# Twenty-eight instead of twenty-four half slabs of expert weights queued behind attention units 0 to 19

## The chip, the cores and the metric

One Trainium2 chip, and one of its cores. The core has five engines that run side by side: TensorE (PE, with its weight loads as PEld), VectorE (DVE), ScalarE (ACT), GpSimd (POOL) and SyncE (SP), which here issues all DMAs. Sixteen DMA engines move the data between the chip's memory and SBUF. The metric is the device time of one execution in microseconds, as the median of several runs; less is better.

## The reference

Three stages, one behind the other: a linear attention with decay over blocks of 64, a soft mixture of experts in which 32 slots go through 8 experts, and a layer of the form g(x w_in) w_out with g(h) = h - tanh(h).

```python
def _attn_ref(q, k, v, lam):               # 4 x 8 heads x 768 x 64
    for b in range(nb):                    # 12 blocks of 64
        intra = (qb @ kb^T * Dmask) @ vb
        inter = (qb * lam_pow) @ kv_state
        out[:, :, sl] = intra + inter
        kv_state = lam_block * kv_state + (kb * rev_pow)^T @ vb

def _moe_ref(x, phi, w1, w2):              # x 3072 x 512, w1 8 x 512 x 1024, w2 8 x 1024 x 512
    logits = x @ phi                       # 3072 x 32
    d = softmax of logits over the tokens
    slot_input = d.T @ x
    for e in range(E):                     # 4 slots each
        slot_out[e] = max(slot_input[e] @ w1[e], 0) @ w2[e]
    return softmax of logits over the slots @ slot_out

def _moe2_ref(x, w_in, w_out):             # 512 x 2048, 2048 x 512
    h = x @ w_in
    return (h - tanh(h)) @ w_out
```

## The kernel before

**Attention.** Queries are taken in 24 units: chunk c of 128 positions (six of them) and batch b (four), u = 4c + b, all eight heads at once. A unit needs a tile of q and k (`qk`, 512 KB, L237), one of v (256 KB, L244) and, for 14 of the units, one of k turned (256 KB, L242); for the six units of `TURN_K` TensorE makes the turned k itself (L250), and the last chunk needs none. `scores(u)` multiplies q and k (L285), `attend(u)` applies them to v and adds the state's part (L302, L309), and updates the state (L318). `route(u)` turns the result for the experts' routing (L343), and routing sums run along with the attention. Three buffers each hold `qk`, `v` and `k`.

**Order.** The program is written in the order in which each engine runs it. Pass u of the loop issues `qk` of unit u + 3, then `fill(FILL[u])`, then k and v of unit u + 3; it holds the scores of unit u + 1 and the attend of unit u. SP is one queue in program order: an issue that has to wait for a buffer holds up everything behind it. The v of unit u + 3 uses the buffer of unit u, so it waits for unit u's attend. A DMA also waits for the one that was issued eight before it to land.

**Expert weights.** There are 32 tiles of 1 MB (two of w1 and two of w2 for each of the 8 experts), each loaded by two DMAs of 512 KB, called halves here. `fill(n)` queues up to n halves, in the order of the experts, as long as a ring has a free tile. The rings: `a` with 3 tiles and `b` with 12, there from the start; `d` with one, in memory that is free once the state is no longer updated (opened behind pass 19); `e` with one, in that of `qk` (opened behind pass 22); `c` with 4, in the rest of the attention's memory (opened at its end). So at most 30 halves can be queued before pass 20, 32 before pass 23. Behind the attention, a tile that an expert has used is filled again (`freed`), with the later experts' weights and then with slabs of w_in and w_out.

**Experts and main stage.** For each expert e, `expert1(e)` (L576, names `hp<-w`) multiplies the slots by w1, and `expert2(e - 1)` (L600, `op<-w`) the earlier expert's hidden values by w2. Then slabs of w_in and w_out, which come as 64-bit numbers (`wi`, `wo`, 512 KB a load), are decoded by GpSimd (`top`, L117) and VectorE (`wif`, `wf`, L121), and the main stage works through 96 chunks with TensorE, ScalarE and VectorE (L795 to L828). The slabs go through ring `a` of three tiles, so that a load there waits for an earlier slab's decode.

Of the kernel before, what the change touches and what calls it, by code (L numbers as in the profile page):

```python
# [63 lines left out]
LINEAR = 43, 47  # L64
CHECK = 57, 59, 63
TURN_K = [0, 1, 2, 6, 11, 16]
FILL = [2, 1, 1, 2, 1, 1, 1, 1, 1, 1, 2, 1, 1, 1, 1, 2, 1, 1, 1, 1, 3, 3, 6, 8]
RING = dict(a=3, b=12, d=1, e=1, c=4)
RING_OF = "a" * 3 + "b" * 12 + "de" + "c" * 4 + "a" * 3 + "b" * 8

# [2 lines left out]
def tile_main(ctx, tc, qkv, lam, phi, w1, w2, w_in, w_out, out):  # L73
# [107 lines left out]
    def fill(most=100):  # L181
        while most and (half or weight_loads and free[ring_next()]):
            if half:
                next(half[0])
                half.pop()
            else:
                f, *a = weight_loads.pop()
                steps = f(*a)
                next(steps)
                half.append(steps)  # L190
            most -= 1
# [18 lines left out]
    with pool("att_out") as att_out:  # L210
# [226 lines left out]
        for u in range(-1, NU):  # L437
            if 3 <= u + 3 < NU:
                load_unit(u + 3, 0)
            if u >= 0:  # L440
                fill(FILL[u])
            if 3 <= u + 3 < NU:
# [705 lines left out]
```

## Time and profile before

| | |
|---|---|
| median of 3 runs | 317.36 us (317.2 to 318.54) |
| profiled execution, its own time | 314.61 us |
| its span | 312.8 us |
| TensorE busy | 294.9 us (94%) |
| VectorE, ScalarE, GpSimd busy | 180.8, 134.0, 111.8 us |
| moved by DMA | 79.77 MB, mean 255 GB/s |
| chain that ended last, by engine | PE 55%, DMA 27%, DVE 8%, issue 4% |
| granted TensorE clock, mean | 0.994 of full speed |

The profile is of one execution, in microseconds from the start of its span; 1.8 us of its time lie outside the span. The attention runs to about 108 us, the routing's end to 116, the experts to 157, the main stage from there to the end. The share of busy time on TensorE is high in all of them, since its instructions are pipelined and their ends are modelled, so what a stage waits for is to be read from the instructions themselves. A DMA share is the mean over the core's 16 DMA engines and can come out a little over 1 in a short stretch.

### The profile page before, as it was taken

The page shows a single profiled execution, that of the slowest core. Times are in us where ns is not written, and L with a number is a line of the kernel's source. Part 1 is how long each engine was busy: PE and PEld are TensorE (multiplying, and loading weights), DVE is VectorE, ACT ScalarE, POOL GpSimd, SP SyncE. Part 2 cuts the span into 40 slices and gives each one's busy share as a digit, 9 for nine tenths or more (in the row PEclk, how much of TensorE's full clock was granted, in tenths as well). Part 3 has the DMA queues.
Part 4 walks back from the last instruction along what each step waited for, and adds up shares of the span by engine and source line. Part 5 has one row for each costly group of instructions (what it writes and reads, how often), then busy time and mean ns, then how long its engine had stood idle before and what let it go on. Part 6 is the DMA issues. An engine that isn't in the chain of part 4 may idle for free.

```text
span 312.8 us, 7421 instructions
## 1 busy us (share of the span) xinstructions
PE 294.9 (94%) x2999; PEld 213.3 (68%) x2999; DVE 180.8 (58%) x329; ACT 134.0 (43%) x280; POOL 111.8 (36%) x163
## 2 busy tenths in 40 slices
PE   8989999999999999997989889999999899999991
PEld 7868787878787774442366567777754677787771
DVE  4844444554544244510069758597772877968782
ACT  1434333233433423321249578586633544454420
POOL 3346766577573014010376345677500001000000
PEclk9999999999999999999999999999999999999997
DMA  6999999999999999999999847563000030303254
GB/s 202 375 397 389 396 377 327 394 369 316 404 336 376 395 402 399 394 397 400 392 348 324 312 148 272 176 237 127 2 2 0 2 134 0 134 2 134 81 188 141
DMA packets 33255, 79.77 MB, mean 255 GB/s; under 512 B 3648, under 2 KB 3904, under 8 KB 33216
## 3 DMA queue, kind: packets, MB, share of 16 engines
q1 hardware_dynamic: 33216, 79.25, 68.8%
q8 instruction: 25, 0.41, 0.5%
q14 instruction: 14, 0.11, 0.1%
HBM read 72.95 MB, written 6.29 MB: 253 GB/s over the span
## 4 chain that ended last, share of the span: by engine, by line
PE 55%; DMA 27%; DVE 8%; issue 4%; POOL 1%; SPq 1%; ACT 1%; DVEq 0%; POOLq 0%; ACTq 0%
PE ops L820 22%; DMA w<-in_w 16%; DMA qk<-in_qkv 7%; PE dps L795 6%; PE sc L285 6%; PE xp L309 5%; DMA wi<-in_w_in 3%; DVE r L813 3%; PE xnp L343 3%; PE xp L302 3%; PE up L318 2%; DVE part L828 2%; PE ops L1056 1%; PE ap L387 1%; PE qp L872 1%
## 5 line engine op out<-in xcount | busy, mean ns | idle before, releaser
L820 PE MATMUL ops<-wr,r 128*128 128x512 f32 (+1 forms) x388 | 109.0, 397 | 1.2 <-ACT part L826 0.9
L820 PEld LDWEIGHTS ops<-wr,r 128*128 128x128 f32 x388 | 72.3, 188 | 22.2 <-ACT part L826 3.1
L799 ACT ACTIVATE s<-dps 128x512 f32<-128x512 f32 x96 | 56.9, 603 | 53.8 <-PE dps L795 51.5
L813 DVE SCALAR_TENSOR_TENSOR r<-dps,mt,s 128x512 fp32r<-128x512 f32 x89 | 64.9, 746 | 19.7 <-ACT s L799 18.9
L795 PE MATMUL dps<-c,ms 128*128 128x512 f32 x96 | 39.5, 425 | 3.8 <-DVE r L813 1.9
L289 DVE TENSOR_TENSOR at<-sc,dtab 128x512 f32<-128x512 f32 x48 | 30.9, 684 | 13.9 <-PE sc L285 13.9
L257 POOL TENSOR_TENSOR qs<-qk,ql 128x512 f32<-128x512 f32 x20 | 25.8, 1288 | 30.0 <-DMA qk<-in_qkv 26.5
L345 ACT COPY xn<-xnp 128x512 f32<-128x512 f32 x24 | 14.1, 586 | 41.7 <-PE xnp L343 41.7
L285 PE MATMUL sc<-qk 64*128 64x128 f32 x384 | 27.9, 285 | 1.8 <-DMA qk<-in_qkv 1.7
L285 PEld LDWEIGHTS sc<-qk 64*128 64x128 f32 x384 | 23.3, 187 | 8.1 <-issue 5.0
L795 PEld LDWEIGHTS dps<-c,ms 128*128 128x128 f32 x96 | 17.9, 188 | 15.2 <-DVE r L813 7.4
L309 PE MATMUL xp<-at,v 128*64 128x128 f32 x384 | 26.3, 279 | 0.0
L264 POOL TENSOR_TENSOR kc<-k,dtab 128x512 f32<-128x512 f32 x20 | 21.2, 1059 | 12.7 <-PE up L318 5.5
L312 ACT COPY xt<-xp 128x256 f32<-128x256 f32 x48 | 17.8, 373 | 16.5 <-PE xp L309 16.0
L309 PEld LDWEIGHTS xp<-at,v 128*64 128x64 f32 x384 | 20.5, 136 | 4.1 <-issue 3.8
L324 DVE TENSOR_TENSOR st<-up,sd 128x256 f32<-128x256 f32 x16 | 6.8, 425 | 26.0 <-PE up L318 23.7
L828 DVE TENSOR_TENSOR part<-ops,part 128x512 f32<-128x512 f32 (+1 forms) x29 | 17.9, 665 | 0.9 <-PE ops L1056 0.9
L576 PE MATMUL hp<-w,si 128*32 128x256 f32 x256 | 16.1, 383 | 2.4 <-DMA w<-in_w 2.4
L600 PE MATMUL op<-w,hz 128*32 128x512 f32 x128 | 16.5, 594 | 0.0
L117 POOL CAST top<-wo 128x512 f16<-128x512 bf16 x16 | 14.9, 953 | 4.2 <-DMA wo<-in_w_out 2.2
L117 POOL CAST top<-wi 128x512 f16<-128x512 bf16 x16 | 14.1, 896 | 6.2 <-DMA wi<-in_w_in 5.6
L121 DVE SCALAR_TENSOR_TENSOR wif<-wi,top 128x512 uint32<-128x512 uint32 x16 | 13.2, 833 | 5.4 <-POOL top L117 5.4
(181 smaller groups left out, 340.7 us busy)
## 6 DMA issues: line engine op xcount, KB each, us to landing
w<-in_w SPq DMA_DIRECT2D x64, 512.0 KB, 9.9
qk<-in_qkv SPq DMA_DIRECT2D x24, 512.0 KB, 7.2
wi<-in_w_in SPq DMA_DIRECT2D x16, 512.0 KB, 4.8
wo<-in_w_out SPq DMA_DIRECT2D x16, 512.0 KB, 4.3
v<-in_qkv SPq DMA_DIRECT2D x24, 256.0 KB, 6.4
out<-part SPq DMA_DIRECT2D x23, 256.0 KB, 2.2
k<-in_qkv SPq DMA_DIRECT2D x14, 256.0 KB, 7.8
out<-part SPq DMA_DIRECT2D x2, 128.0 KB, 3.5
```

What stands on the lines that cost most here:

```text
L117: nc.gpsimd.tensor_copy(out=every(top().bitcast(F16), 2, 1)[:, sl], in_=every(raw().bitcast(BF16)[:, 4:], 4, 0)[:, sl])
L257: nc.gpsimd.tensor_tensor(out=qs_t[u], in0=qk_t[u][:, 0], in1=ql, op=ALU.mult)
L264: nc.gpsimd.tensor_tensor(out=kc_t[u], in0=k_t.pop(u).rearrange("p (h d) -> p h d", h=H), in1=kd, op=ALU.mult)
L285: nc.tensor.matmul(sc[h2][:, p], qk[sl, 1, p], qk[sl, 0, p], start=True, stop=True)
L289: nc.vector.tensor_tensor(out=by_head(at_t[u], h2), in0=sc[h2], in1=by_head(dtab, h2), op=ALU.mult)
L309: nc.tensor.matmul(at_head(p, h2), v[:, h * DH:(h + 1) * DH], at[:, h], start=c == 0 and p < 2, stop=True, skip_group_check=True)
L312: nc.scalar.copy(xt_t[u][:, h2], xp[h2])
L795: nc.tensor.matmul(d_t[n], ms[:, f * P:(f + 1) * P], c4[:, c], start=True, stop=True)
L799: nc.scalar.activation(out=s, in_=d_t[n], func=AF.Square, scale=math.sqrt(1.0 / 3))
L813: nc.vector.scalar_tensor_tensor(out=r_t[n], in0=d, scalar=mt[:, f, NS:], in1=s, op0=ALU.add, op1=ALU.mult)
L820: nc.tensor.matmul(op, r_t[n][:, t * P:(t + 1) * P], wr_t[f // 2][:, f % 2, sl], start=first, stop=last)
L828: nc.vector.tensor_tensor(out=pt, in0=op, in1=pt, op=ALU.add)
```

## The change

One table changes: how many halves each pass may queue. The sum of the first twenty passes goes from 24 to 28: pass 3 queues one fewer, passes 5, 6, 13, 17 and 19 one more each, and pass 21 is allowed two instead of three. Passes 20 to 22 queued the last eight of the first 32 halves (three, three, two); now pass 20 queues three, pass 21 one and pass 22 none, because the rings are full.

```diff
 TURN_K = [0, 1, 2, 6, 11, 16]
-FILL = [2, 1, 1, 2, 1, 1, 1, 1, 1, 1, 2, 1, 1, 1, 1, 2, 1, 1, 1, 1, 3, 3, 6, 8]
+FILL = [2, 1, 1, 1, 1, 2, 2, 1, 1, 1, 2, 1, 1, 2, 1, 2, 1, 2, 1, 2, 3, 2, 6, 8]
 RING = dict(a=3, b=12, d=1, e=1, c=4)
```

Which half of which tile a pass loads shifts along, and with it the numbers in the tiles' names. Nothing moves on the other engines. The rows below are SP's queue in program order; in a name such as `w2_0_1_407`, 2 says w2, 0 the expert, 1 the tile, and the last number is the buffer's. `L237` loads q and k, `L242` the turned k, `L244` v, `L156` and `L165` halves of w1 and w2.

SP in passes 5 and 6, from q and k of unit 8 to those of unit 10, before:

```order
L237 DMA qk_502<-in_qkv 128x1024
L165 DMA w2_0_1_407<-in_w2 128x2x512
L242 DMA k_505<-in_qkv 128x512
L244 DMA v_507<-in_qkv 128x512
L237 DMA qk_576<-in_qkv 128x1024
L156 DMA w1_1_0_578<-in_w1 128x1024
L242 DMA k_580<-in_qkv 128x512
L244 DMA v_582<-in_qkv 128x512
L237 DMA qk_641<-in_qkv 128x1024
```

The same stretch after:

```order
L237 DMA qk_500<-in_qkv 128x1024
L165 DMA w2_0_1_502<-in_w2 128x2x512 x2
L242 DMA k_505<-in_qkv 128x512
L244 DMA v_507<-in_qkv 128x512
L237 DMA qk_576<-in_qkv 128x1024
L156 DMA w1_1_0_578<-in_w1 128x1024 x2
L242 DMA k_581<-in_qkv 128x512
L244 DMA v_583<-in_qkv 128x512
L237 DMA qk_642<-in_qkv 128x1024
```

Each pass queues two halves instead of one between a load of q and k and the next one.

SP in passes 17 to 20, from the weights of pass 17 on, before:

```order
L165 DMA w2_2_0_1314<-in_w2 128x2x512
L244 DMA v_1409<-in_qkv 128x512
L237 DMA qk_1478<-in_qkv 128x1024
L165 DMA w2_2_1_1480<-in_w2 128x2x512
L244 DMA v_1482<-in_qkv 128x512
L237 DMA qk_1541<-in_qkv 128x1024
L165 DMA w2_2_1_1480<-in_w2 128x2x512
L244 DMA v_1544<-in_qkv 128x512
L237 DMA qk_1603<-in_qkv 128x1024
L156 DMA w1_3_0_1605<-in_w1 128x1024 x2
L156 DMA w1_3_1_1608<-in_w1 128x1024
```

After:

```order
L165 DMA w2_2_1_1317<-in_w2 128x2x512
L156 DMA w1_3_0_1412<-in_w1 128x1024
L244 DMA v_1414<-in_qkv 128x512
L237 DMA qk_1483<-in_qkv 128x1024
L156 DMA w1_3_0_1412<-in_w1 128x1024
L244 DMA v_1486<-in_qkv 128x512
L237 DMA qk_1545<-in_qkv 128x1024
L156 DMA w1_3_1_1547<-in_w1 128x1024 x2
L244 DMA v_1550<-in_qkv 128x512
L237 DMA qk_1609<-in_qkv 128x1024
L165 DMA w2_3_0_1611<-in_w2 128x2x512 x2
L165 DMA w2_3_1_1614<-in_w2 128x2x512
```

Passes 17 and 19 queue two halves instead of one, and the weights run four halves ahead by then; in pass 20 the first half of the second w2 tile of expert 3 (ring `d`) stands ahead of the last v, where a half of w1 of that expert stood.

## Rows read from the trace of the kernel before

**Rows 1.** Chain of waits, in order of time: start us, us, what.

```profile
55.25 8.25 DMA qk<-in_qkv
63.55 1.16 PE sc L285 x16
...
146.37 10.65 DMA wi<-in_w_in
157.07 0.87 POOL top L117
```

**Rows 2.** TensorE, experts 6 and 7: start, us, engine, line, operation, names, count, [idle before].

```profile
140.20 1.93 PE L576 MATMUL hp<-w,si 128*32 128x256 f32 x32
141.96 1.90 PE L600 MATMUL op<-w,hz 128*32 128x512 f32 x16
...
144.28 0.38 PE L588 MATMUL ht<-cst,hr 128*128 128x128 f32 x2
145.21 0.64 PE L576 MATMUL hp<-w,si 128*32 128x256 f32 x8 [0.55 <-DMA w<-in_w]
...
149.41 1.90 PE L600 MATMUL op<-w,hz 128*32 128x512 f32 x16
```

**Rows 3.** Stretches: us, busy of five engines, granted clock, DMA share, GB/s.

```profile
18.00:45.00 27.00, 25.45 (x463) 20.91 (x460) 11.84 (x24) 8.87 (x23) 16.97 (x18) 1.00 1.03 389
45.00:51.00 6.00, 6.00 (x103) 4.40 (x98) 2.51 (x5) 3.33 (x11) 5.04 (x6) 1.00 0.88 316
...
69.00:78.00 9.00, 9.00 (x168) 7.65 (x168) 4.00 (x8) 3.25 (x7) 6.81 (x8) 1.00 0.95 312
78.00:90.00 12.00, 12.00 (x227) 9.50 (x215) 6.29 (x13) 4.86 (x14) 6.72 (x8) 1.00 1.03 399
90.00:99.00 9.00, 9.00 (x170) 7.63 (x168) 3.94 (x9) 3.15 (x10) 5.01 (x5) 1.00 0.92 328
99.00:156.00 57.00, 54.09 (x649) 28.52 (x645) 16.68 (x50) 16.73 (x40) 9.27 (x29) 1.00 1.04 397
```

**Rows 4.** SP's waits: engine, line, releaser: us in total, times, longest.

```profile
SPq L244 <- PE up L318: 34.4, 19, 3.4
```

**Rows 5.** SP: issues of q and k for units 10, 20, 21, 23.

```profile
37.48 0.42 SPq L237 DMA_DIRECT2D qk<-in_qkv  x1
...
81.80 0.42 SPq L237 DMA_DIRECT2D qk<-in_qkv  x1
...
85.72 0.38 SPq L237 DMA_DIRECT2D qk<-in_qkv  x1
...
94.24 0.61 SPq L237 DMA_DIRECT2D qk<-in_qkv  x1
```

**Rows 6.** DMA issues: KB, us to landing; rows 5's four, then 107.7 and 162.4 us.

```profile
qk<-in_qkv SPq DMA_DIRECT2D x1, 512.0 KB, 7.2
...
qk<-in_qkv SPq DMA_DIRECT2D x1, 512.0 KB, 7.7
...
qk<-in_qkv SPq DMA_DIRECT2D x1, 512.0 KB, 7.0
...
qk<-in_qkv SPq DMA_DIRECT2D x1, 512.0 KB, 6.0
...
w<-in_w SPq DMA_DIRECT2D x1, 512.0 KB, 8.4
...
wi<-in_w_in SPq DMA_DIRECT2D x1, 512.0 KB, 3.9
```

**Rows 7.** TensorE: first scores of units 10, 20, 21 and 23.

```profile
45.53 1.16 PE L285 MATMUL sc<-qk 64*128 64x128 f32 x16
...
89.94 1.16 PE L285 MATMUL sc<-qk 64*128 64x128 f32 x16
...
93.71 1.16 PE L285 MATMUL sc<-qk 64*128 64x128 f32 x16
...
102.72 1.16 PE L285 MATMUL sc<-qk 64*128 64x128 f32 x16
```

## The prediction

> **What bounds the kernel now.** I read the chain of waits first, then TensorE's instructions at the end of the expert stage, then the DMA share by stretch, then the landing of single loads.
>
> The chain runs on TensorE through the attention, with a few loads of q and k in it: the load issued at 55.25 landed 8.25 us later, and the scores started 0.05 us after that [rows 1]. So a load's time to landing counts from the start of its issue, and the attention's operands sometimes come last already. Behind the attention the chain is DMA up to 157 us: the first slab of w_in, issued at 146.37, landed 10.65 us later and released the first decode [rows 1].
>
> TensorE gives the other view of that place. Expert 6 goes through its first product and on to the next in 1.76 us (140.20 to 141.96); expert 7, whose turn came with the transposes at 144.28, reached the same point at 149.41, after four waits on weights, the first of 0.55 us [rows 2]. Up to expert 6 the stage runs at TensorE's pace, and at expert 7 TensorE catches up with the DMA. Without waits expert 7 would have started 0.31 us behind the transposes (as expert 6 did behind its own) and been through at 144.28 + 0.31 + 1.76 = 146.35. **At most 149.41 - 146.35 = 3.06 us are to be had there**, and only if both sides come earlier: the weights, and TensorE itself.
>
> The DMA had room in the attention and none behind it. The share is 1.03 to 1.04 where the queue is full (389 GB/s in 18 to 45 us, 399 in 78 to 90, 397 in 99 to 156), and there are three dips: 0.88 and 316 GB/s, 0.95 and 312, 0.92 and 328 [rows 3]. SP doesn't look far ahead: 19 loads of v wait for the state update of an earlier unit, 34.4 us in sum [rows 4], and all that SP issues later stands behind them. If little is queued per unit, the DMA runs dry.
>
> **The change, part by part.** It computes nothing new. 64 halves of weights are loaded before and after; a half costs 0.524 MB / 397 GB/s = 1.32 us of DMA [rows 3]. Against the kernel before, SP is one half behind after pass 3, level after pass 5, one ahead from pass 6, two from 13, three from 17, four from 19, and level again at pass 22. A half that pass u adds goes out behind the q and k of unit u + 3 and ahead of those of unit u + 4.
>
> *Pass 3's half taken out.* The queue is full there, so the half moves to pass 5 for nothing: 0. No scores stall that this could free; the loads for units 6 to 8 land earlier than needed.
>
> *Four halves ahead.* Two prices have to be found: how much the DMA makes up in the dips (what the end of the weights gains), and how long TensorE stands still for late q and k. For the second, the slack of a load is the start of its scores less its issue less its time to landing: unit 10 has 45.53 - 37.48 - 7.2 = 0.85 us, unit 20 0.44, unit 21 0.99, unit 23 2.48 [rows 5 to 7]. Read in the same way, units 17, 18, 19 and 22 have 2.07, 1.50, 1.17 and 1.15, unit 11 with its transposes 0.96, and unit 14 none [rows 1].
>
> How much a dip takes is not shown by any row; two readings bound it. By bytes, against 389 GB/s, the dips lose 6 x 73/389 = 1.13, 9 x 77/389 = 1.78 and 9 x 61/389 = 1.41 us. By DMA share, against 1.035, they are free for 0.90, 0.74 and 1.00 us [rows 3].
> - By bytes: pass 6's half makes unit 10 wait 1.32 - 0.85 = 0.47, and the other 0.85 goes in the first dip. Pass 13's half goes in the second, behind slacks of 2.07 and 1.50. Pass 17's makes unit 21 wait 1.32 - 0.99 = 0.33; the 0.99 left and pass 19's 1.32 are under unit 23's slack once the last dip has taken 1.41. Stalls 0.80; made up 0.85 + 1.32 + 1.41 = 3.58.
> - By share: 0.47 again; of pass 13's half 0.58 stays, which unit 20 feels by 0.14; then 0.44 + 1.32 - 0.99 = 0.77 at unit 21; the rest, 2.31 - 1.00 = 1.31, is under 2.48. Stalls 1.38; made up 0.85 + 0.74 + 1.00 = 2.59.
>
> I take 1.2 us of stalls, nearer to the share, since that is the row that says whether a DMA engine was free. The Trainium skill speaks against that choice ("Perfetto Trace Analysis", Identifying the Most-Contended Engine): it wants the bytes, since the occupancy of 16 DMA engines misleads. By it the stalls would be 0.8 and the gain 0.4 us more; here bytes and share dip in the same three places and differ in depth.
>
> *The rings.* By pass 22 both kernels have queued 32 halves, and the next go out when attention memory is free. SP then stands with less behind it. Before, the first load past the attention's end took 8.4 us to land; one that found little queued took 3.9 [rows 6]. So there are 4.5 us of queue to use up, against 3.58 + 0.80 or 2.59 + 1.38: it doesn't run dry, by little. The sixteenth tile, now asked for in pass 20, waits for the last state update, which was over before the v ahead of it could go out: 0.
>
> *Sum.* TensorE starts the experts 1.2 us later (0.80 to 1.38), runs through expert 7 without the waits, and is 3.06 - 1.2 = 1.9 us earlier behind it (1.68 to 2.26). The weights and w_in, 2.6 to 3.6 us ahead, allow that. What is late next is the decode: it starts from the same w_in load and TensorE's next product, both moved, and from there slab loads wait for decoded slabs, so all shifts together. On the profiled execution 314.61 becomes 312.7; the median of the runs is 317.36, 2.75 above, and becomes **315.5 us**.
>
> **The rivals.**
>
> *No room.* The dips are not idle in the sense that counts, and nothing is made up. Then each half ahead is paid where the slack ends: 0.47 at unit 10, 0.85 at unit 14, 0.15, 0.73 and 0.77 at units 19 to 21, 2.97 in sum. Expert 7 no longer waits, since TensorE is that much later itself: 3.06 - 2.97 = 0.1, and the weights land when they did. 317.3 us. For it: with a share of 0.88 to 0.95 most engines are busy in a dip, and a load has landed only when its last part has. Against it: bytes fall by 16 to 20% there. The Trainium skill bears on it ("DMA: Bandwidth & Descriptors", Why a DMA increments its semaphore by 16 and not by 1): up to 16 engines finish independently and only the full count means landed. By that, a dip in the mean may hide one late engine; no row here tells the engines apart.
>
> *Slower.* Every half ahead is paid in full on TensorE: a stall delays the attend, the attend delays the v that SP waits for [rows 4], and the next q and k go out as late as the stall was long, so no slack returns. Price 4 x 1.32 = 5.28, less 3.06: 2.2 us, 319.6 us. It decides from stalls over 3.06 us; over 4.65 it can be measured. Against it: the loads of units 22 and 23 had 1.15 and 2.48 us left, and a stalled TensorE gives the queue time to drain.
>
> *It changes nothing at the end*, because the queue runs dry at the attention's end and the halves gained are lost again. Price: 317.4. The 4.5 us speak against it; I count it with no room.
>
> **How the numbers follow.** About 0.5% (1.6 us) is what a measurement here can tell from no change. Forecast, stalls of 0.80 to 1.38: 0.45, and its times, 315.1 to 315.7, are just faster by that. No room, the dry queue, and stalls between 1.5 and 4.6: 0.38, all within 0.5%. Slower: 0.17. So faster 0.45, same 0.38, slower 0.17. The range runs from 314.6, where only unit 10 stalls (3.06 - 0.47 gives 314.8) with a little for the spread of the runs, to 318.8, inside the slower case; about 1 in 20 lies below, 3 in 20 above.
>
> **What would show it.** Right: the three dips filled to a share near 1.03; the scores of units 10 and 21 waiting for q and k, with 0.8 to 1.4 us more of that in sum; expert 0 starting that much later; no wait on weights in expert 7; the first w_in slab landing over 2 us earlier. No room: dips as before, or filled with the landings no denser, and stalls near 3 us. Wrong altogether: stalls over 3 us, or a gap in the DMA at 105 to 112 us, or the 1.9 us present at 157 and gone by the first outputs.

## The result and the profile after

The kernel after took 314.39 us (313.24 to 315.38, 4 executions) beside 317.49 us (317.2 to 318.54, 4) for the kernel before: a ratio of 0.9895 [0.9848, 0.9943]. Two further comparisons of 12 executions each gave 315.20 beside 316.48 us, 0.9973 [0.9935, 1.001], and 315.14 beside 316.41, 0.9971 [0.9933, 1.0009]. Over all executions the medians are 315.11 us (28, from 311.9 to 317.7) and, beside all the experiments but without the four of the first comparison, 316.55 us (121, from 313.3 to 319.93). So the change is worth about 1.4 us or 0.45%, less than half of what the first comparison shows. Ratios here leave out executions more than 1.5% above their kernel's fastest; medians and the counts by clock further below are over all executions.

The first median lies 0.2 us below the range that was given, the median of all 28 lies 0.4 us below the forecast of 315.5. That nearness says little: the profiled execution on which the sum rests was not like most, and larger errors nearly cancel, as the last part shows.

The profiled execution of the kernel after took 315.38 us (span 313.6), which is *more* than the 314.61 of the one before. Two executions decide nothing; what they show is where the time lies. First the DMA in the three dips of [rows 3], by the stretches of the kernel after (us, busy of the five engines, granted clock, DMA share, GB/s):

```profile
45.00:51.00 6.00, 5.63 (x105) 4.75 (x105) 2.77 (x5) 2.94 (x10) 3.57 (x4) 1.00 1.01 382
69.00:78.00 9.00, 8.43 (x146) 7.02 (x144) 4.18 (x7) 3.25 (x7) 4.16 (x6) 1.00 1.04 383
90.00:99.00 9.00, 8.40 (x169) 7.07 (x165) 3.94 (x9) 2.51 (x6) 4.29 (x5) 1.00 1.01 390
```

The dips are gone: 316, 312 and 328 GB/s have become 382, 383 and 390. Where they were, TensorE now stands a little. Four of the scores that wait for q and k, of units 9, 10, 17 and 21, in TensorE's order of time (start, us, engine, line, operation, names, count, [idle before]):

```profile
41.22 1.16 PE L285 MATMUL sc<-qk 64*128 64x128 f32 x16 [0.31 <-DMA qk<-in_qkv]
46.42 1.16 PE L285 MATMUL sc<-qk 64*128 64x128 f32 x16 [0.35 <-DMA qk<-in_qkv]
77.87 1.16 PE L285 MATMUL sc<-qk 64*128 64x128 f32 x16 [0.57 <-DMA qk<-in_qkv]
95.71 1.16 PE L285 MATMUL sc<-qk 64*128 64x128 f32 x16 [0.60 <-DMA qk<-in_qkv]
```

Their sum up to 118 us, from the waits of the kernel after (us in total, times, longest):

```profile
PE sc L285 <- DMA qk<-in_qkv: 4.2, 7, 1.0
```

In the kernel before that sum is 1.7 us in 3 waits. Of the difference, 2.5 us, 0.69 is a wait of unit 0's scores, which delays nothing (they start at 6.08 us, beside 6.06 before); the other 1.8 us are most of what reaches the experts. TensorE's expert 0, expert 7 and first product of the main stage, kernel after:

```profile
117.81 1.93 PE L576 MATMUL hp<-w,si 128*32 128x256 f32 x32
...
146.29 0.38 PE L588 MATMUL ht<-cst,hr 128*128 128x128 f32 x2
146.60 1.30 PE L576 MATMUL hp<-w,si 128*32 128x256 f32 x16
148.54 0.64 PE L576 MATMUL hp<-w,si 128*32 128x256 f32 x8 [0.64 <-DMA w<-in_w]
149.83 0.64 PE L576 MATMUL hp<-w,si 128*32 128x256 f32 x8 [0.65 <-DMA w<-in_w]
150.29 1.90 PE L600 MATMUL op<-w,hz 128*32 128x512 f32 x16
...
159.11 1.10 PE L743 MATMUL mp__2401<-wif,so 128*32 128x128 f32 x16
```

and the first and the last of these places in the kernel before:

```profile
115.80 1.93 PE L576 MATMUL hp<-w,si 128*32 128x256 f32 x32
...
158.23 1.11 PE L743 MATMUL mp__2401<-wif,so 128*32 128x128 f32 x16
```

Expert 0 starts 117.81 - 115.80 = 2.01 us later. Expert 7 has two waits on weights, 1.29 us, instead of the four of [rows 2], and the stretch from expert 0 to the main stage is 41.30 us long instead of 42.43. From there to the end of the span it is 154.5 us in this execution and 154.6 in that one, and between 154.1 and 155.2 in every trace of this study: what stands at the main stage's first product stands at the end, to within about 1 us. So two marks tell nearly the whole time of a trace, the start of expert 0 (called E below) and the start of the main stage (M).

Two repeats of the kernel after came out better in their traces: E 116.33 and M 155.75 (no wait left in expert 7), and E 117.48 and M 157.36 (one wait of 0.30 us). The first of them is of the fastest of the 28 executions, 311.9 us.

Why weights still come late in this trace, though SP is four halves ahead, shows at the attention's end. The stretch of 108 to 118 us, before:

```profile
108.00:118.00 10.00, 9.79 (x118) 7.01 (x116) 3.38 (x16) 2.87 (x11) 1.93 (x6) 1.00 1.04 399
```

and after, its first 8 us in pieces of 2 us:

```profile
108.00:110.00 2.00, 2.00 (x36) 1.63 (x36) 0.00 (x0) 1.20 (x3) 0.00 (x0) 1.00 0.79 305
110.00:112.00 2.00, 2.00 (x42) 1.68 (x41) 0.36 (x2) 0.72 (x2) 0.00 (x0) 1.00 0.69 233
112.00:114.00 2.00, 1.79 (x16) 1.27 (x18) 1.22 (x7) 1.53 (x6) 0.00 (x0) 1.00 0.92 268
114.00:116.00 2.00, 2.00 (x19) 1.19 (x11) 0.91 (x3) 0.55 (x3) 0.00 (x0) 1.00 0.85 237
```

The queue has run low: 233 to 305 GB/s for 8 us, where the kernel before moves 399. SP's waits say what it stood at. Between 100 and 125 us, after (engine, line, releaser: us in total, times, longest):

```profile
SPq L156 <- DMA v<-in_qkv: 5.9, 2, 5.6
SPq L156 <- PE hp L576: 4.3, 1, 4.3
SPq L165 <- PE op L600: 2.8, 1, 2.8
```

Before, most of SP's waiting there is for a weight load issued eight earlier to land, that is, for a full queue:

```profile
SPq L165 <- DMA w<-in_w: 6.9, 8, 1.0
SPq L156 <- DMA w<-in_w: 5.3, 7, 0.9
SPq L156 <- PE xp L309: 2.5, 1, 2.5
SPq L156 <- PE hp L576: 0.7, 1, 0.7
```

After, SP stands because memory isn't free: all the halves that rings `a`, `b` and `d` hold, 32, are queued early, the next place is the attention's (the 5.6 us end when the last v has landed), and then that of tiles which TensorE has yet to use (4.3 and 2.8 us). The chain of waits of the kernel after runs through just that place (start us, us, what):

```profile
108.69 1.05 PE xp L309 x16
109.80 0.33 SPq L156
...
113.35 0.62 SPq L156
114.01 12.22 DMA w<-in_w
126.25 10.52 DMA w<-in_w
136.78 10.44 DMA w<-in_w
147.24 10.65 DMA wi<-in_w_in
```

From the last attend over SP's issues into four loads, of which the last is the first slab of w_in. Set beside [rows 1], that slab is issued 0.87 us later than before and takes the same 10.65 us.

### The profile page after: what moved, and what is told of

It reads as the page before. It is cut to its first block, busy times and chain, and to the rows that moved or that the text cites. A ratio compares the mean times of both kernels' runs of the same rounds, so it can differ in the third digit from the quotient of the medians.

```text
span 313.6 us, 7419 instructions
## 1 busy us (share of the span) xinstructions
PE 294.5 (94%) x2999; PEld 212.6 (68%) x2999; DVE 181.2 (58%) x329; ACT 133.9 (43%) x280; POOL 112.9 (36%) x163
## 4 chain that ended last, share of the span: by engine, by line
PE 44%; DMA 36%; DVE 9%; issue 4%; SPq 3%; POOL 1%; ACT 1%; DVEq 0%; POOLq 0%; ACTq 0%
PE ops L820 21%; DMA w<-in_w 19%; DMA qk<-in_qkv 12%; PE dps L795 5%; DVE r L813 4%; DMA wi<-in_w_in 3%; PE xp L309 3%; PE sc L285 3%; DVE part L828 2%; PE xp L302 2%; PE xnp L343 1%; PE ops L1056 1%; PE qp L872 1%; POOL top L117 1%; DMA wo<-in_w_out 1%
```

## The experiments

Two theories went into the first runs: the *handover* (the gain is made at expert 7 and at most 3.06 us, less the stalls in the attention) and rivals in which the gain lay elsewhere, above all in executions unlike the profiled one.

### Both kernels again

No edit: the kernel before three more times, one execution each, and the kernel after twice more, 12 executions each.

> The kernel before once more, for a trace from the chip that times the others. Theory A (the profile of before is typical, and what the change gains is at most the 3.06 us that expert 7 waits): 314.6 us as in its profile or 317.5 as timed, with the three dips in the DMA share and 2.4 us of waits on weights in expert 7 in either case. Theory B (the profile of before was one of its better executions): about 317.5 us, and the 3 us more lie where the DMA decides, as a longer wait of expert 7 on its weights (over 4 us) or as later q and k in the attention.

> The kernel before, for a trace of a common execution: the two at hand took 314.3 and 314.6 us, while its median is 316.5 to 317.5. Theory C (the DMA is later in the common executions, by the 2 to 3 us that leaving out expert 7's loads gave over the 3.06 us ceiling): an execution over 316 us has waits on weights over 4 us in expert 7, or waits in expert 6 as well, and later stages as long as in the others. Theory D (the spread lies in the main stage or elsewhere): the first product of the main stage starts at about 158 us in it as well.

> As the run before it, another execution: the same two theories. With both traces the time of the execution less the start of the main stage's first product should be 154 to 155 us plus the 1.8 us outside the span under theory C, whatever the execution's time.

> The changed kernel once more, with the kernel before on the same chip. Theory A (handover at expert 7, gain at most 3.06 us less the stalls in the attention): ratio 0.992 to 1.000. Theory B (before waits longer than its profile shows): ratio 0.985 to 0.992. Either: the DMA share falls under 1 at about 108 to 116 us, where SP waits for the attention's memory and for expert 0.

> The changed kernel a third time, beside the kernel before: the two comparisons so far gave 0.9895 and 0.9973 with intervals that meet at 0.994. Theory A and C together (3.06 us less the stalls, and 1 to 2 us more where before waits longer): 0.988 to 0.995. Theory A alone: 0.993 to 0.997.

The kernel after came out at ratios of 0.9973, within what the handover gives, and 0.9971, at the weak end of what was expected. Two of the executions of the kernel before, of 314.3 and 314.97 us, are like its profile (M 158.18 and 158.41). The other took 317.65 us, nearer to the median of its timed executions, and differs at expert 7, not in the main stage. TensorE in it, around expert 7:

```profile
146.84 0.64 PE L576 MATMUL hp<-w,si 128*32 128x256 f32 x8 [1.92 <-DMA w<-in_w]
148.03 0.64 PE L576 MATMUL hp<-w,si 128*32 128x256 f32 x8 [0.55 <-DMA w<-in_w]
149.31 0.88 PE L576 MATMUL hp<-w,si 128*32 128x256 f32 x8 [0.64 <-DMA w<-in_w]
150.60 1.08 PE L576 MATMUL hp<-w,si 128*32 128x256 f32 x8 [0.41 <-DMA w<-in_w]
151.45 2.66 PE L600 MATMUL op<-w,hz 128*32 128x512 f32 x16
...
161.03 1.07 PE L743 MATMUL mp__2401<-wif,so 128*32 128x128 f32 x16
```

and by stretches, the columns as in [rows 3]:

```profile
144.00:149.00 5.00, 2.20 (x26) 0.98 (x22) 0.19 (x1) 0.60 (x1) 0.00 (x0) 1.00 1.03 402
149.00:150.00 1.00, 0.69 (x8) 0.16 (x8) 0.00 (x0) 0.00 (x0) 0.00 (x0) 0.78 1.04 383
150.00:153.00 3.00, 2.60 (x20) 0.79 (x20) 0.00 (x0) 0.47 (x1) 0.00 (x0) 0.50 1.06 387
```

M is 161.03, 2.80 us later than in the profile of before, in two parts. The weights land some 1.65 us later (the last quarter of the product starts at 150.60 instead of 148.95; the four waits are 3.52 us in sum, where over 4 were expected). And TensorE, which was busy for 2.20 of the 5 us ahead, falls to half its clock, 0.50 of full speed or 1.2 GHz of 2.4, in 150 to 153 us: the quarters take 0.88 and 1.08 us instead of 0.64 and the next product 2.66 instead of 1.90. That is the other 1.15 us. In the profile of before, the clock was 1.00 in the same stretch:

```profile
150.00:153.00 3.00, 3.00 (x29) 0.93 (x18) 0.19 (x1) 0.79 (x2) 1.85 (x2) 1.00 1.05 384
```

The Trainium skill ("TensorE: Matmul & The Clock Gate", HAM oscillation — how this bites in real kernels) describes this: a wait for DMA between bursts of products drops the clock to half, and what follows starts slow. This trace agrees, with 0.50.

The mean granted clock of each timed execution shows how common that is. Of 121 executions of the kernel before, 39 had a clock of 0.993 or more and a median of 314.97 us; 82 were below (0.982 to 0.992) and had 317.25 us. Traces without the fall read 0.994 or more, the one with it 0.991; the border is mine. Of 28 executions of the kernel after, 26 were above it, with a median of 315.11 us. So the profiled execution of the kernel before belonged to the third with the higher clock, and measured by that third alone (314.97 beside 315.11) the change gains nothing. Both groups are picked by their outcome, so their distance of 2.3 us is not the price of the clock alone: a longer wait and a fallen clock come together.

### The ceiling: expert 7 without its weights

Expert 7 multiplies by expert 6's tiles, which are there, and its own 8 halves are not loaded; expert 6's tiles are given back behind expert 7. Once on the kernel before, with a repeat, and once on the kernel after.

```diff
@@ expert_loads @@
-    for e in range(NE):
+    for e in range(NE - 1):
...
-                w = w1_t[e, k // 2]
+                w = w1_t[min(e, NE - 2), k // 2]
...
-                    op[g * NS:(g + 1) * NS], hz_t[e % 3][:, q], w2_t[e, q // 4][:, g],
+                    op[g * NS:(g + 1) * NS], hz_t[e % 3][:, q], w2_t[min(e, NE - 2), q // 4][:, g],
```

> The kernel before with expert 7's weights not loaded: expert 7 uses expert 6's tiles, so 8 halves (10.5 us of DMA) are left out and the output isn't the reference's. The attention is as before, so no stalls are added. Theory A: expert 7 waits for nothing, the slabs of w_in are there in time, and the gain is the whole ceiling: 3.06 us, ratio 0.990. If the ceiling was read wrong and the DMA decides all the way into the main stage: over 5 us faster. If the decode or something else is behind the wait at expert 7: under 1.5 us.

> The kernel before without expert 7's loads (expert 7 uses expert 6's tiles, so the output isn't the reference's), a second time, as the base of the next run: 311.5 us again, with no execution at a clock under 0.993.

> The changed kernel without expert 7's loads, in the same way. Behind the attention the DMA has 10 us to spare in both, so the difference of this run to the one before it is the price of the stalls in the attention alone. Sum of the prediction: 0.8 to 1.4 us, about 312.7 us. If the timed executions of the changed kernel lose their gain to stalls: 2.5 to 3.5 us, 314 to 315 us. If they lose it to the dry queue at the attention's end: 0.8 to 1.4 us here, while the changed kernel itself takes 315.1.

On the kernel before: 311.52 us, 0.9829 [0.9786, 0.9873], and 311.95 us, 0.9881 [0.9835, 0.9928]; over all 12 executions 311.82 (310.78 to 312.85), the clock at 0.993 or more in all; of the 52 executions of the kernel before that were timed beside them, 16 had such a clock. On the kernel after: 313.94 us, 0.9937 [0.9901, 0.9974]. TensorE in the first of them:

```profile
115.49 1.93 PE L576 MATMUL hp<-w,si 128*32 128x256 f32 x32
...
143.97 0.38 PE L588 MATMUL ht<-cst,hr 128*128 128x128 f32 x2
144.28 1.93 PE L576 MATMUL hp<-w,si 128*32 128x256 f32 x32
146.03 1.90 PE L600 MATMUL op<-w,hz 128*32 128x512 f32 x16
...
154.86 1.07 PE L743 MATMUL mp__2389<-wif,so 128*32 128x128 f32 x16
```

Expert 7 now runs like expert 6. M comes 3.37 us earlier than in the profile of before; E came 0.31 earlier, and the rest is 3.06 us, the ceiling that the prediction worked out. From E to M it is 39.37 us when nothing waits.

But the medians differ by 316.55 - 311.82 = 4.73 us, not 3.06 (by 5.6 and 4.4 us, each run beside the kernel before on its own chip). In the executions that are timed, the place costs half as much again as in the profiled one. The runs on both kernels also give the price of the change in the attention, with expert 7 out of the account: 313.94 - 311.82 = 2.12 us, which lies between what was expected of either theory. What is left over is 315.11 - 313.94 = 1.17 us, the loss that the kernel after still has through expert 7's loads (timed on other chips). By the way they are formed, these add up to the gain: 4.73 - 2.12 - 1.17 = 1.44 us. The two costs are loosely known: drawing the executions anew at random gives 0.8 to 3.2 us for the first and -0.1 to 2.6 for the second (4.4 to 5.3 for the 4.73).

### The clock by itself

The kernel before, and the three-halves version from the next section, with nine small products that nobody reads between the quarters of expert 7's first product. They give TensorE something to do while it waits.

```diff
                 w = w1_t[e, k // 2]
+                if e == NE - 1:
+                    keep_warm(2 if k else 3, 0)
```

> The kernel before, with TensorE kept at work while expert 7 waits for its weights: three dummy products ahead of its first weights and two ahead of each of the other three, into a bank that is free there. The loads and their order are as before. Clock theory (in the common executions of before TensorE's clock falls to half behind the wait at expert 7, which a trace showed as 0.50 from 150 to 153 us, and that costs some 2 us on top of the wait): 1.5 to 2.3 us faster, about 315.0 us, with a mean granted clock of 0.993 or more in nearly all executions. If the later weights, not the clock, make the common executions long: no change, 316.5 us. If the dummies come in the way: up to 1 us slower.

> Three halves ahead in passes 8, 13 and 19, with the dummy products at expert 7. If its gain is both the handover and the clock, the clock is already held and the dummies add nothing: 312.8 to 313.2 us, as without them. If a part of its executions still falls in clock: up to 0.5 us faster than without.

On the kernel before, 11 of 12 executions now hold the clock (11 of 29 without the edit, beside it). The median went from 316.35 to 315.35 us, less than the 1.5 to 2.3 that were expected, and the ratio, 0.9988 [0.9958, 1.0017], can't tell it from 1. The trace shows late weights by themselves, the clock held (first quarter, first product of the main stage, and a stretch):

```profile
146.55 0.64 PE L578 MATMUL hp<-w,si 128*32 128x256 f32 x8 [0.67 <-DMA w<-in_w]
...
159.67 1.11 PE L745 MATMUL mp__2414<-wif,so 128*32 128x128 f32 x16
150.00:153.00 3.00, 3.00 (x29) 0.99 (x28) 0.00 (x0) 0.47 (x1) 1.01 (x2) 1.00 1.05 384
```

The weights are nearly as late as in the trace with the fallen clock (146.55 beside 146.84, and 145.21 in the profile of before), and M, 159.67, is 1.36 us earlier than there and 1.44 later than in the profile. So the clock's fall costs about 1 us of the 4.73, by the medians and by the traces, which leaves, by difference, some 0.7 us beyond the 3.06 for later weights. Where nothing waits, the same products cost their own time, which was not expected: 315.46 us instead of 313.23 for the three-halves version, 2.2 us, some 0.25 each. TensorE there, around expert 7:

```profile
145.40 0.93 PE L616 MATMUL wp<-c 128*128 128x512 f32 x3
146.27 0.64 PE L578 MATMUL hp<-w,si 128*32 128x256 f32 x8
146.84 0.73 PE L616 MATMUL wp<-c 128*128 128x512 f32 x2
147.50 0.64 PE L578 MATMUL hp<-w,si 128*32 128x256 f32 x8
```

No wait is left between them, and each pair shifts the next quarter by 0.66 us. As a repair the products are no match for weights that come in time.

### How many halves, and where

The table is the only edit; p81319b and p81319c repeat p81319. The sum of the first twenty passes less 24 is how many halves a table is ahead. In words: h25 has the first three moves of the change (passes 3, 5 and 6) and h26 pass 13's too; p1319, p81319 and p4 add one half each in the passes they are named for (p4: 8, 13, 18 and 19) and leave pass 3 alone; h30 adds passes 8 and 18 to the kernel after.

```diff
-FILL = [2, 1, 1, 2, 1, 1, 1, 1, 1, 1, 2, 1, 1, 1, 1, 2, 1, 1, 1, 1, 3, 3, 6, 8]
+FILL = [2, 1, 1, 1, 1, 2, 2, 1, 1, 1, 2, 1, 1, 1, 1, 2, 1, 1, 1, 1, 3, 3, 6, 8]  # h25
+FILL = [2, 1, 1, 1, 1, 2, 2, 1, 1, 1, 2, 1, 1, 2, 1, 2, 1, 1, 1, 1, 3, 3, 6, 8]  # h26
+FILL = [2, 1, 1, 2, 1, 1, 1, 1, 1, 1, 2, 1, 1, 2, 1, 2, 1, 1, 1, 2, 3, 3, 6, 8]  # p1319
+FILL = [2, 1, 1, 2, 1, 1, 1, 1, 2, 1, 2, 1, 1, 2, 1, 2, 1, 1, 1, 2, 3, 3, 6, 8]  # p81319
+FILL = [2, 1, 1, 2, 1, 1, 1, 1, 2, 1, 2, 1, 1, 2, 1, 2, 1, 1, 2, 2, 3, 3, 6, 8]  # p4
+FILL = [2, 1, 1, 1, 1, 2, 2, 1, 2, 1, 2, 1, 1, 2, 1, 2, 1, 2, 2, 2, 3, 2, 6, 8]  # h30
```

> One half ahead: pass 3's extra half moved to pass 5, and one more in pass 6; the rest as before (25 halves by pass 19). Theory A: the first dip takes 0.85 us of it, unit 10 waits 0.5 us, the weights come 0.9 us earlier: 0.9 us faster, ratio 0.997. Linear theory (each half ahead is worth its 1.32 us of DMA up to the fourth): 0.8 us faster, a quarter of the whole. No-room theory: 0 to 0.5 us slower.

> Two halves ahead: as the run with 25, and one more in pass 13 (26 halves by pass 19). Theory A: the second dip takes most of it, 1.6 to 2.2 us of weights ahead and 0.5 us of stalls: 1.6 to 2.2 us faster, ratio 0.993 to 0.995, that is as good as the whole change. Linear theory: half of the whole change, 1.6 us. No-room theory: 0.5 to 1 us slower.

> Two halves ahead, put where the loads had most slack before: one more in pass 13 (units 17 and 18 had 2.07 and 1.50 us) and one more in pass 19 (unit 23 had 2.48 us); pass 3 as before, 26 halves by pass 19. Theory A (gain is the smaller of 3.06 us less the stalls and what the dips make up): stalls 0 to 0.2 us, made up 1.3 to 2.6 us, no dry queue: 1.3 to 2.6 us faster, ratio 0.992 to 0.996, as good as the whole change. Linear theory (each half 0.8 us): 1.6 us faster. If the first dip and pass 6 are what counts: nothing.

> Three halves ahead: as the run before it, and one more in pass 8, behind unit 11's q and k and ahead of unit 12's, which had 1.6 us; 27 halves by pass 19. Theory A: stalls 0 to 0.4 us, made up 2.2 to 3.6 us: at the ceiling of 3.06 us less stalls, 2.2 to 3.0 us faster, ratio 0.990 to 0.993. Linear theory: 2.5 us faster. Dry-queue theory (what is made up beyond two halves is lost at the attention's end): no better than with 26, and the DMA share under 1 in 108 to 118 us.

> Three halves ahead, in passes 8, 13 and 19, a second time, on one chip with the changed kernel. If the places decide: 0.985 to 0.992, and 0.3% or more under the changed kernel of the same call. If only the number of halves ahead counts: within 0.2% of it.

> Three halves ahead in passes 8, 13 and 19 once more, on one chip with the run with four: 312.8 to 313.2 us, ratio 0.987 to 0.991.

> Four halves ahead as in the changed kernel (28 by pass 19), but in passes 8, 13, 18 and 19, with pass 3 left alone. If the number decides (the queue runs dry at the attention's end with four ahead, since the rings hold no more): about 1 us slower than with three, 314 to 315 us, and a DMA share well under 1 in 108 to 118 us. If the places decide (the changed kernel loses to stalls behind passes 6 and 17): as good as three, 312.5 to 313.3 us.

> Six halves ahead: as the changed kernel, with one more in passes 8 and 18 (30 halves by pass 19, all that the rings hold there). Theory A: the dips are full, so the two more are paid in TensorE's stalls, 2 to 3.5 us of them in sum, and are lost in a dry queue of over 2 us at the attention's end, which comes later: 0 to 1.5 us slower than before. Linear theory: 4.9 us faster. No-room theory: 2 to 5 us slower.

| kernel | halves ahead | E, us | M - E, us | GB/s in 108 to 118 us | median, us | ratio | clock held |
|---|---|---|---|---|---|---|---|
| before | 0 | 115.80, 115.79, 116.11 | 42.43, 42.39, 42.30 | 399 | 316.55 | | 39 of 121 |
| h25 | 1 | 116.18 | 41.61 | 398 | 314.95 | 0.9975 [0.994, 1.001] | 11 of 12 |
| h26 | 2 | 116.86 | 39.55 | 394 | 313.24 | 0.994 [0.9903, 0.9977] | 11 of 12 |
| p1319 | 2 | 116.03 | 41.13 | 398 | 313.83 | 0.9911 [0.988, 0.9942] | 11 of 12 |
| p81319 (three runs) | 3 | 116.68, 117.01, 116.34 | 40.32, 39.72, 39.79 | 391, 356, 386 | 313.23 | 0.9877, 0.9891, 0.9921 | 23 of 24 |
| after (three runs) | 4 | 117.81, 116.33, 117.48 | 41.30, 39.42, 39.88 | 284, 364, 256 | 315.11 | 0.9895, 0.9973, 0.9971 | 26 of 28 |
| p4 | 4 | 119.07 | 39.37 | 288 | 314.94 | 0.9955 [0.9919, 0.9992] | 11 of 12 |
| h30 | 6 | 117.32 | 40.15 | 252 | 314.11 | 0.993 [0.9895, 0.9966] | 12 of 12 |

E and M are of one trace per run; the traces of before leave out the one with the fallen clock (E 116.06, M - E 44.97). The intervals of the three-halves version are [0.9832, 0.9922], [0.9849, 0.9932] and [0.9889, 0.9953].

Four things follow. *The first halves carry nearly all of the gain*: two or three ahead reach 313.2 to 313.8 us, and one is enough for the clock to hold in 11 of 12 executions. *The fourth half costs more than it brings*, wherever it is queued: two tables with four, after and p4, which share only passes 13 and 19, come out at 315.11 and 314.94, and beside three halves on one chip at 315.14 and 312.77, and at 314.94 and 313.72. *The drop of the DMA at the attention's end goes with the number*: with up to three halves ahead it moves 356 to 399 GB/s in 108 to 118 us, with four or six 252 to 364. *It is not a price per half*: six ahead are not shown to be slower than four (314.11 and 315.11), and are faster than before.

That the drop is what the fourth half costs is not shown. M - E above 39.4 us, which is what late weights leave at expert 7, doesn't follow it: 0.0 in p4 at 288 GB/s, 0.9 in the first trace with three halves at 391. In the mean of the traces the fourth half costs nothing there (M - E 39.99 us with four halves, 39.94 with three) and 1 us in the attention (E 117.67 and 116.68), though single traces lie as far apart as that. A part of it that nobody had counted is the last v, which stands behind pass 20's weights. TensorE's last attend waits for it in three of the five traces with the halves of after or p4, 0.33, 0.38 and, in p4, 1.22 us, and in none of the others:

```profile
109.90 1.09 PE L309 MATMUL xp<-at,v 128*64 128x128 f32 x16 [1.22 <-DMA v<-in_qkv]
```

Of the expectations, the one for six halves missed (0 to 1.5 us slower than before, and they are faster), the three-halves version first came out better than expected (0.9877, beside 0.990 to 0.993) and at its last repeat a little worse (313.72 us, beside 312.8 to 313.2), and p1319 better (0.9911, beside 0.992 to 0.996).

The three-halves version, passes 8, 13 and 19, beats both kernels: 313.23 us, 3.3 us below the kernel before and 1.9 below the kernel after by medians over all executions. At expert 7 its three traces have one wait each left, of 0.64, 0.15 and 0.22 us.

## Why the prediction was right and wrong

**The bound and its place: right, for the profiled execution.** The 3.06 us at expert 7 came out as 3.06 in the run without expert 7's weights, and everything from the main stage on shifts with M.

**The step from the profiled execution to the median: wrong, and the main miss.** "On the profiled execution 314.61 becomes 312.7; the median of the runs is 317.36, 2.75 above, and becomes 315.5" carries the offset over as a constant, so that the median can gain no more than the 3.06 us of the profile less the stalls. It is not a constant: it goes with expert 7's loads. Without expert 7's loads the median, 311.82 us, is that of its profiled executions (311.97 and 312.16), and no clock is under 0.993. The ceiling for the median was 4.73 us (in the first comparison the gain alone was 317.49 - 314.39 = 3.10, more than this step allowed before any stall), and the offset of the kernel after is gone (its profiled executions took 315.38, 311.9 and 314.0 us, its median is 315.11). That the offset is the later weights and the fallen clock of the one trace is argued from the executions' clocks. The hint was there before: a profiled execution of 314.61 us below all three timed ones, and the prediction used the difference as a sum to add.

**The stalls: right in the mean of the traces, open for the timed executions.** The term was 1.2 us (0.80 to 1.38). E is 115.94 us in the mean of four traces of before and 117.20 in four with the table of after (the one without expert 7's weights among them): 1.26, with single traces from 0.4 to 1.9. In the timed executions the price is 2.12, which is too loosely known to be told from it. The units named, 10 and 21, do wait in the first trace (0.35 and 0.60), but so do 17, which was given 2.07 us of slack, and 9. In the other three traces unit 10 waits once, unit 21 twice, unit 20 once, and the last v, which the sum left out, is late in two. The rule of the Trainium skill ("Perfetto Trace Analysis", Identifying the Most-Contended Engine), to go by bytes and not by occupancy, would have made the stalls 0.80; here the mean of the traces, 1.26, is nearer to the 1.38 of the share.

**The rings: wrong.** "It doesn't run dry, by little" had 4.5 us of queue against 4.0 to 4.4 us of halves made up and stalls. The DMA did drop, to 233 GB/s in 110 to 112 us, which is the gap that the prediction named as a sign of being wrong altogether. The 4.5 us was the difference of two landings, which says how much lay ahead of one load; it took no account of what SP waits for next. Being four halves earlier, SP reaches the loads that need the attention's memory, and then the freed tiles of expert 0, when TensorE is late by its stalls: 5.6, 4.3 and 2.8 us of waits. In the first trace this comes back at expert 7, where 1.9 us of M - E above 39.4 are left and the first w_in slab, expected over 2 us earlier, is issued 0.87 later. In the two repeats the queue drops too, but 0.0 and 0.5 us are left and the slab is issued 2.5 and 0.9 us earlier. So the gap is shown, and its price is not.

**Pass 3's half for nothing: not contradicted.** The table that has it (h26, with pass 3's half moved) and the one that hasn't (p1319) are about as fast, 313.24 and 313.83; neither isolates it. Against it stands that unit 9, right behind pass 5's extra half, waits 0.31 us in the first trace of after; in the other traces with that half it doesn't.

**The rivals.** *No room* falls: the dips filled to 382 to 390 GB/s, and the weights did come earlier. *Slower* falls, by four and by six halves. *The dry queue* came in part: the DMA drops at the attention's end, but the gain is not lost with it, and what it costs is open. What no rival named is that the clock takes part, and that one half is enough to hold it in 11 of 12 executions.

By medians, the nearness of 315.5 to 315.11 is thus three errors that nearly cancel: a ceiling too low by 1.67 us (4.73 instead of 3.06), costs too low by 2.09 (2.12 + 1.17 instead of 1.2), and a median of before too high by 0.81 (317.36 instead of 316.55).

**Open.** Why most timed executions of before are like one of its four traces and not like the other three; whether the stalls cost more in timed executions than in traces; what the drop at the attention's end costs, and why six halves are no worse than four. That the late weights of one trace stand for all 82 executions with a low clock is argued from their clocks and times, and was not shown; 39 of them have a lower mean clock than that trace's 0.991.

## What to carry to other kernels

Ask first whether the profiled execution is a typical one: where its time or its clock differs from the median of the runs, the difference may lie in the very wait that is to be removed, and then it may not be added as a constant. Prefetch just far enough for the one wait that ends last; past that, a further load can cost more in the stage it is queued in than it brings (here the fourth half), and comes to stand before memory that isn't free yet. To find that number, cut the wait out altogether once (here 311.82 us): what is left above it tells what further prefetch could still bring.

## What the hardware showed that was not expected

- TensorE's clock can fall to 1.2 GHz behind a handful of short waits: 1.92, 0.55, 0.64 and 0.41 us in expert 7, and 0.50 granted in 150 to 153 us. With 0.55, 0.55, 0.64 and 0.64 us in another execution of the same program it stayed at 1.00 there. By the mean clock, and this is argued, 82 of 121 executions land on the slow side.
- Nine products of 128 x 512 in the gaps kept the clock up in 11 of 12 executions and cost 2.2 us where there was no gap.
- A DMA queue that seemed nearly full in the dips (share 0.88 to 0.95) took on more when more was queued: 382 to 390 GB/s at a share of 1.01 to 1.04, where it had been 312 to 328.
